# Attention ahead of the mixers instead of among them, with key chunks taken in twos

## The chip, the cores and the metric

The kernel runs on one core of a Trainium2 chip. The metric is the device time of one execution in microseconds. TensorE (PE) does matrix products into PSUM, VectorE (DVE), ScalarE (ACT) and GpSimd (POOL) work on elements, and SP's queue issues most DMAs.

## The reference

Four batches, eight heads, 768 queries and keys of 64 elements; then a mixer over tokens and channels.

```python
q_assign = np.argmax(np.einsum('bhsd,hcd->bhsc', q_n, c_n), axis=-1)
k_assign = np.argmax(np.einsum('bhsd,hcd->bhsc', k_n, c_n), axis=-1)
mask = q_assign[:, :, :, None] == k_assign[:, :, None, :]
scores = np.where(mask, scale * np.matmul(q, k.transpose(0, 1, 3, 2)), -1000000000.0)
attn = np.exp(scores - np.max(scores, axis=-1, keepdims=True))
attn = attn / (np.sum(attn, axis=-1, keepdims=True) + 1e-09)
x = np.matmul(attn, v)            # then (B,H,S,D) -> (B, S, H*D), D = 512
h = np.maximum(x.transpose(0, 2, 1) @ w_tok1, 0.0) @ w_tok2     # 768 -> 256 -> 768
u = x + h.transpose(0, 2, 1)
out = u + np.maximum(u @ w_ch1, 0.0) @ w_ch2                    # 512 -> 1536 -> 512
```

Here q_n, k_n and c_n are q, k and the 16 centroids of each head, each scaled to length one. The mixer's weights arrive as 64-bit floats, of which the kernel reads two 32-bit words.

## The kernel before

The work unit of attention is a pair `g`: one batch and two heads, 16 pairs in all. `load(g)` brings q and k of the pair in 32 DMAs of 24 KB and v in one, all on SP's queue and two pairs ahead. `turn` (L242) transposes q and k on VectorE into `qkT`, `route_products` (L251) multiplies them with the centroids, `route` (L264) finds each row's first greatest centroid as a one-hot row, and `route_turn` (L291) transposes these on TensorE into `ohT`.

A pair has 12 steps: two halves of the queries (384 columns) by six chunks of 128 keys. A step's `scores` (L312) adds two products into one PSUM tile `sc`: the one-hot rows of queries and keys in bf16, scaled so that a pair of different clusters gets -2**33, and the f32 scores. The two heads lie in two halves of the array's rows (64x128 tiles). ScalarE makes the exp `ex`. Two steps later `values` (L328) multiplies `ex` with v into `av`, the two heads in two halves of the array's columns (128x64 tiles), and VectorE adds `ex` to `sum`. There are two `sc` tiles of two banks each. At a half's end `normalise` (L354) sums over the partitions with a product by ones (`den`), takes the reciprocal of all 128x384 elements, multiplies the transposed output `xT` with it, and GpSimd gathers the largest sums and reciprocals in `worst`. `turn_x` (L374) transposes `xT` on TensorE into `x`.

The mixer of a batch is cut into items. When the four pairs of a batch are done, its items go into `fill`, and `gap()` issues some of them after each later attention step, so that mixer b runs among the steps of batch b+1; the last mixer runs alone. `tok1` (L409) and `tok2` (L423) are the token products, `ch1` (L438) and `ch2` (L452) the channel products; `ch2` adds u by products with an identity (L459).

The weights come in 31 pieces, 512 or 384 KB each, one or two per step from the start. `weight_round` (L162) makes f32 of the two words in five VectorE operations, one of ScalarE and two of GpSimd.

At the end a count of partitions in which sums and reciprocals stayed in range is loaded into the engines' registers; a branch goes to a general version of the kernel if any did not. On this data it isn't taken.

The order in which each engine gets its instructions is the order in which the code is written.

## Time and profile before

| | us |
|---|---|
| runs of the kernel before | median 1219.48 (1219.26 to 1219.65, 3 runs) |
| profiled execution | 1218.17 |
| its span, first to last instruction | 1216.4 |
| TensorE busy | 1046.0 |
| VectorE busy | 532.8 |
| ScalarE busy | 253.2 |
| GpSimd busy | 199.5 |

The profiled execution is one run; what lies outside the span (1.8 us) is launch and end. Busy times of engines overlap in time. TensorE's clock has two levels, 1.2 and 2.4 GHz; the granted clock of a stretch is its mean, 1.00 for the higher one throughout.

### The profile page before, as it was taken

The numbers are of one execution on the slowest core, as the hardware profiler recorded it, in microseconds if no ns is written. First come the engines' busy times: TensorE is split into PE (matmuls) and PEld (weight loads), VectorE is DVE, ScalarE is ACT, GpSimd is POOL, SyncE is SP. The second block draws the span as 40 slices with busy tenths as digits, with TensorE's granted clock in tenths as the row PEclk, the third lists the DMA queues.
The fourth block names the chain that finished last, engine by engine and source line by source line (L and its number), as shares of the span: only waits on it lengthen the run. The fifth ranks groups of instructions, "written<-read, shape, count | busy, mean of one in ns | idle before, by whom it ended". The sixth has DMA issues, their size and how long they took to land.

```text
span 1216.4 us, 10935 instructions
## 1 busy us (share of the span) xinstructions
PE 1046.0 (86%) x4227; PEld 461.8 (38%) x4227; DVE 532.8 (44%) x639; ACT 253.2 (21%) x374; POOL 199.5 (16%) x168
## 2 busy tenths in 40 slices
PE   0425344589999999999999999999999999999997
PEld 0102111133444444444444444444444444455553
DVE  3459989988443325333444334344433243120000
ACT  0212212144222122212222122222221221000000
POOL 0135646522011001011111111110110011000000
PEclk9767667699999999999999999999999999999999
DMA  2342332232020011021100020121000000000000
GB/s 48 109 117 86 80 115 87 61 62 47 11 39 1 26 28 26 1 57 35 30 10 22 9 48 1 24 51 19 14 1 16 11 1 1 26 1 9 18 1 29
DMA packets 118972, 41.74 MB, mean 34 GB/s; under 512 B 107776, under 2 KB 111872, under 8 KB 118912
## 3 DMA queue, kind: packets, MB, share of 16 engines
q1 hardware_dynamic: 118912, 40.96, 14.0%
q8 instruction: 35, 0.57, 0.2%
q14 instruction: 25, 0.20, 0.0%
HBM read 34.64 MB, written 6.29 MB: 34 GB/s over the span
## 4 chain that ended last, share of the span: by engine, by line
PE 73%; DVE 12%; SPq 10%; ACT 2%; DMA 1%; issue 1%; DVEq 0%; ACTq 0%
PE pc L438 21%; PE po L452 21%; PE sc L320 10%; SPq L132 9%; PE av L336 8%; PE pu L423 4%; PE ph L409 3%; DVE wh L175 2%; DVE wh L178 2%; PE po L459 2%; DVE sum L347 1%; DVE wT L188 1%; PE den L362 1%; DVE wh L183 1%; PE px L381 1%
## 5 line engine op out<-in xcount | busy, mean ns | idle before, releaser
L438 PE MATMUL pc<-xT,wc 128*128 128x384 f32 x768 | 265.0, 493 | 0.0
L452 PE MATMUL po<-wc,h 128*128 128x512 f32 x576 | 260.9, 600 | 0.0
L325 ACT ACTIVATE ex<-sc 128x768 f32<-128x768 f32 x192 | 155.4, 810 | 441.7 <-PE sc L320 439.9
L438 PEld LDWEIGHTS pc<-xT,wc 128*128 128x128 f32 x768 | 140.2, 190 | 114.4 <-issue 26.4
L336 PE MATMUL av<-ex,va 128*64 128x384 f32 x768 | 175.1, 536 | 0.0
L320 PE MATMUL sc<-qkT 64*128 64x384 f32 x768 | 168.2, 518 | 0.0
L452 PEld LDWEIGHTS po<-wc,h 128*128 128x128 f32 x576 | 104.9, 190 | 134.0 <-issue 133.5
L347 DVE TENSOR_TENSOR sum<-sum,ex 128x768 f32<-128x768 f32 x128 | 140.1, 1094 | 18.2 <-ACT ex L325 13.8
L371 POOL TENSOR_TENSOR worst<-worst,rcp 128x384 f32<-128x384 f32 x32 | 42.9, 1339 | 632.4 <-DVE rcp L366 632.4
L389 DVE TENSOR_SCALAR h<-pc 128x384 f32<-128x384 f32 x48 | 26.7, 557 | 236.6 <-PE pc L438 236.6
L366 DVE RECIPROCAL rcp<-den 128x384 f32<-128x384 f32 x32 | 81.8, 2556 | 97.9 <-PE den L362 97.9
L320 PE MATMUL sc<-ohT 64*128 64x384 bf16 x384 | 68.6, 353 | 23.2 <-ACT ex L325 22.6
L336 PEld LDWEIGHTS av<-ex,va 128*64 128x64 f32 x768 | 39.2, 139 | 112.9 <-issue 109.6
L370 POOL TENSOR_TENSOR worst<-worst,sum 128x384 f32<-128x384 f32 x64 | 67.2, 1050 | 88.0 <-DVE sum L347 85.5
L320 PEld LDWEIGHTS sc<-qkT 64*128 64x128 f32 x768 | 75.8, 206 | 0.9 <-issue 0.9
L320 PEld LDWEIGHTS <-ohT 64*128 64x128 bf16 x384 | 19.3, 94 | 136.0 <-issue 133.0
L197 POOL TENSOR_TENSOR wlow<-wlow,wpow 128x512 f32<-128x512 f32 (+1 forms) x31 | 47.0, 1516 | 134.5 <-DVE wpow L192 73.7
L257 PE MATMUL pr<-qkT,cnd 128*32 128x384 f32 x128 | 16.3, 584 | 49.5 <-DVE qkT L246 49.5
L391 ACT ACTIVATE h<-pc 128x384 f32<-128x384 f32 x48 | 23.6, 491 | 165.8 <-PE pc L438 165.8
L381 PE MATMUL px<-ident,xT 128*128 128x128 f32 x96 | 18.4, 304 | 39.1 <-DVE xT L368 26.6
L196 ACT ACTIVATE wlow<-raw 128x512 f32<-128x512 uint32 (+1 forms) x31 | 20.4, 658 | 138.3 <-POOL wc L201 77.2
L175 DVE TENSOR_SCALAR wh<-raw 128x512 uint32<-128x512 uint32 (+1 forms) x31 | 34.8, 1123 | 32.7 <-DMA raw<-in_moe_w_tok_dram 27.6
(68 smaller groups left out, 626.1 us busy)
## 6 DMA issues: line engine op xcount, KB each, us to landing
raw<-in_moe_w_ch_dram SPq DMA_DIRECT2D x24, 512.0 KB, 3.6
qk<-in_q_dram SPq DMA_DIRECT2D x256, 24.0 KB, 2.2
qk<-in_k_dram SPq DMA_DIRECT2D x256, 24.0 KB, 2.2
va<-in_v_dram SPq DMA_DIRECT2D x16, 384.0 KB, 3.3
out_dram<-o SPq DMA_DIRECT2D x24, 256.0 KB, 2.0
raw<-in_moe_w_tok_dram SPq DMA_DIRECT2D x3, 512.0 KB, 5.7
raw<-in_moe_w_tok_dram SPq DMA_DIRECT2D x4, 384.0 KB, 3.2
cen<-in_centroids_dram SPq DMA_DIRECT2D x1, 32.0 KB, 1.8
```

Of the source, the lines that this page charges most:

```text
L132: nc.sync.dma_start(d4[:, i], s4[:, i])
L175: nc.vector.tensor_scalar(out=h, in0=hi, scalar1=0x7FFFFFFF, scalar2=None, op0=ALU.bitwise_and)
L197: nc.gpsimd.tensor_tensor(out=low, in0=low, in1=power.bitcast(F32), op=ALU.mult)
L320: nc.tensor.matmul(sc[:, h, 0:HS], lhsT=src[rows, 1, j], rhs=src[rows, 0, js], start=start, stop=not start,)
L325: nc.scalar.activation(out=ex, in_=sc[:, :, 0:HS], func=ACT.Exp, scale=SM_SCALE)
L336: nc.tensor.matmul(st["av"][h * D : (h + 1) * D], lhsT=st["va"][:, h, j], rhs=ex[:, h], start=(j == 0), stop=(j == NJ - 1),)
L347: nc.vector.tensor_tensor(out=acc, in0=acc, in1=st.pop(("ex", qh, j)), op=ALU.add)
L366: nc.vector.reciprocal(out=rcp, in_=den)
L370: nc.gpsimd.tensor_tensor(out=worst[0], in0=worst[0], in1=acc[:, h], op=ALU.add)
L423: nc.tensor.matmul(pu, lhsT=st["h1"][:, t, f * P : (f + 1) * P], rhs=wt2[:, t, js], start=(t == 0), stop=(t == NT - 1),)
L438: nc.tensor.matmul(pc, lhsT=wc1[:, f, ct * P : (ct + 1) * P], rhs=uT[:, f, HJ * hf : HJ * hf + HJ], start=(f == 0), stop=(f == NF - 1),)
L452: nc.tensor.matmul(st["pf"], lhsT=st["h2"][:, ct, j * P : (j + 1) * P], rhs=wc2[:, ct], start=(ct == 0), stop=False,)
```

## The change

All 16 pairs of attention now come first, then the four mixers one after another. The parts:

- A step is a group `m` of two key chunks (96 groups, six per pair): both chunks' scores, which fill both `sc` tiles, then both chunks' values of two groups before. `work` has 7 `ex` buffers instead of 5.
- `av` is copied once (`avT`) and transposed by `half_turn`; `half_out` divides where `px` leaves PSUM, straight into `x`. Row sums come as 32-row tiles (`half_sums`), VectorE transposes them, and `half_reciprocals` takes 128x6 elements.
- `route` compares with the row's greatest value alone; that each row has one winner is counted in `cells`, from `route_turn`, whose copies both go to ScalarE. `worst` and its sums on GpSimd are gone; `fits` tests the reciprocals after the first batch's mixer and loads three counts there.
- q and k of a pair come in eight DMAs of 96 KB; for the first pair q's go on ScalarE's queue.
- Rounding a weight piece takes three VectorE operations, two of ScalarE and one of GpSimd. One piece is done every four groups; the 12 pieces of `w_ch2` come after attention, beside the first mixer's `ch1`, in memory that attention has left.
- All four batches' `x` are kept. The first batch's `tok1` and `tok2` stand at the end of attention (`ends`). `tok2` adds into `x`, `turn_u` transposes u for `ch1`, and `ch2` adds u on VectorE instead of by identity products. The next batch's token products stand inside the last channel products of the one before.

```diff
-STEPS = 2 * NJ
+GROUPS = NJ
+WEVERY = 4
...
-LAG_V, LAG_D = 2, 4
...
-    def pool(name, bufs, **kw):
-        return fast.enter_context(tc.tile_pool(name=name, bufs=bufs, **kw))
...
-    ps_sc = pool("ps_sc", 2, space=PSUM)
+    def pool(name, bufs, stack=None, **kw):
+        return (stack or fast).enter_context(
+            tc.tile_pool(name=name, bufs=bufs, reuse_waits="tile", **kw)
+        )
+    ps_w = pool("ps_w", 3, space=PSUM)
     ps_av = pool("ps_av", 1, space=PSUM)
-    ps_m = pool("ps_m", 2, space=PSUM)
...
+    ps_sc_stack = fast.enter_context(ExitStack())
+    ps_sc = pool("ps_sc", 2, ps_sc_stack, space=PSUM)
...
+    work = pool("work", 7, attention)
...
+    def load(g, queues=None):
...
-        for a, src in enumerate((q, k)):
+        for a, src in ((1, k), (0, q)):
+            queue = queues[a] if queues else nc.sync
...
-                d4 = st["qk"][c * QP : (c + 1) * QP, a].rearrange("r j i d -> r i j d")
-                for i in range(NQ):
-                    nc.sync.dma_start(d4[:, i], s4[:, i])
+                queue.dma_start(
+                    st["qk"][c * QP : (c + 1) * QP, a].rearrange("r j i d -> r (j i) d"),
+                    src[b, h, :, d0 : d0 + QP].rearrange("(i r j) d -> r j i d", i=NQ, j=NJ),
+                )
...
+        def scalar_part(p):
+            p["h"] = tmp("wh", U32, p["n"])
+            nc.scalar.activation(out=p["h"].bitcast(F32), in_=p["hi"].bitcast(F32), func=ACT.Abs)
+            p["up"] = tmp("wup", I32, p["n"])
+            nc.scalar.activation(out=p["up"], in_=p["lo"], func=ACT.Copy, scale=float(2.0**-29))
...
+            nc.vector.tensor_scalar(
+                out=h.bitcast(F32), in0=h.bitcast(F32), scalar1=TINY, scalar2=HUGE,
+                op0=ALU.max, op1=ALU.min,
+            )
+            nc.vector.tensor_scalar(
+                out=h, in0=h, scalar1=0x07FFFFFF, scalar2=3,
+                op0=ALU.bitwise_and, op1=ALU.logical_shift_left,
+            )
+            T = tmp("wT", U32, p["n"])
+            nc.vector.scalar_tensor_tensor(
+                out=T, in0=p["hi"], scalar=0xC0000000, in1=h,
+                op0=ALU.bitwise_and, op1=ALU.bitwise_or,
+            )
...
+            nc.gpsimd.tensor_tensor(out=dst.bitcast(I32), in0=T, in1=up, op=ALU.add)
...
+        for i in range(len(pieces) + 2):
+            def step(i=i):
+                if 2 <= i:
+                    rest(pieces[i - 2][0], parts[i - 2])
+                if 1 <= i <= len(pieces):
+                    scalar_part(parts[i - 1])
+                if i < len(pieces):
+                    load_bits(pieces[i][1], parts[i])
+            yield step
...
-        ge = small.tile([P, NR, C], F32, name="ge")
-        nc.vector.tensor_tensor(
-            out=ge, in0=sc, in1=mx.unsqueeze(2).to_broadcast([P, NR, C]), op=ALU.is_ge
-        )
-        nc.vector.tensor_tensor(
-            out=ge, in0=ge, in1=ramp.unsqueeze(1).to_broadcast([P, NR, C]), op=ALU.mult
-        )
-        first = small.tile([P, NR], F32, name="first")
-        nc.vector.reduce_max(out=first, in_=ge, axis=AX.X)
         oh = ohs[g % 2].rearrange("p a j (h x) -> p (a j) h x", h=2)[:, :, :, 0:C]
         nc.vector.tensor_tensor(
-            out=oh, in0=ge.rearrange("p (n h) c -> p n h c", h=2),
-            in1=first.rearrange("p (n h) -> p n h", h=2).unsqueeze(3).to_broadcast([P, 2 * NJ, 2, C]),
-            op=ALU.is_equal,
+            out=oh, in0=sc.rearrange("p (n h) c -> p n h c", h=2),
+            in1=mx.rearrange("p (n h) -> p n h", h=2).unsqueeze(3).to_broadcast([P, 2 * NJ, 2, C]),
+            op=ALU.is_ge,
         )
...
-        if a == 0:
+        if a == 1:
...
         if a == 0:
             nc.scalar.copy(out=st["ohT"][:, 0], in_=po)
         else:
-            nc.vector.tensor_scalar(
-                out=st["ohT"][:, 1], in0=po, scalar1=BIG, scalar2=-BIG, op0=ALU.mult, op1=ALU.add
-            )
-    def split(n):
-        g, s = divmod(n, STEPS)
-        return g, s // NJ, s % NJ
-    def scores(n):
-        g, qh, j = split(n)
+            nc.scalar.activation(
+                out=st["ohT"][:, 1], in_=po, func=ACT.Copy, scale=BIG, bias=-BIG,
+                accum_out=cells[:, g : g + 1],
+            )
...
-        sc = ps_sc.tile([P, 2, 512], F32, name="sc")
+        scs = [ps_sc.tile([P, 2, 512], F32, name="sc") for _ in range(2)]
         for src, start in ((st["ohT"], True), (st["T"], False)):
+            for i in range(2):
+                for h in range(2):
+                    rows = slice(h * D, (h + 1) * D)
+                    nc.tensor.matmul(
+                        scs[i][:, h, 0:HS], lhsT=src[rows, 1, j0 + i], rhs=src[rows, 0, js],
+                        start=start, stop=not start,
+                    )
+        for i in range(2):
+            ex = work.tile([P, 2, HS], F32, name="ex")
+            nc.scalar.activation(out=ex, in_=scs[i][:, :, 0:HS], func=ACT.Exp, scale=SM_SCALE)
+            st["ex", qh, j0 + i] = ex
+    def add_up(m):
+        g, qh, j0 = split(m)
+        st = state[g]
+        e = [st["ex", qh, j0 + i] for i in range(2)]
+        if j0 == 0:
+            acc = st["sum", qh] = sums.tile([P, 2, HS], F32, name="sum")
+            nc.vector.tensor_tensor(out=acc, in0=e[0], in1=e[1], op=ALU.add)
+        else:
+            acc = st["sum", qh]
+            for i in range(2):
+                nc.vector.tensor_tensor(out=acc, in0=acc, in1=e[i], op=ALU.add)
+    def values(m):
+        g, qh, j0 = split(m)
+        st = state[g]
+        if j0 == 0:
+            st["av"] = ps_av.tile([P, HS], F32, name="av")
+        for j in (j0, j0 + 1):
+            ex = st.pop(("ex", qh, j))
...
+                    st["av"][h * D : (h + 1) * D], lhsT=st["va"][:, h, j], rhs=ex[:, h],
+                    start=(j == 0), stop=(j == NJ - 1),
                 )
...
+        if j0 == NJ - 2:
+            st["avT", qh] = sums.tile([P, HJ, P], F32, name="avT")
+            nc.scalar.copy(out=st["avT", qh].rearrange("p j t -> p (j t)"), in_=st.pop("av"))
+    def half_sums(hi):
+        g, qh = divmod(hi, 2)
+        st = state[g]
+        acc = st.pop(("sum", qh)).rearrange("p h (j t) -> p (h j) t", j=HJ)
+        den = st["den"] = ps_w.tile([P, 2 * HJ, QP], F32, tag="w", name="den")
+        for i in range(NQ):
+            rows = slice(i * QP, (i + 1) * QP)
+            nc.tensor.matmul(den[rows], lhsT=ones, rhs=acc[:, :, rows], start=True, stop=True)
+    def half_reciprocals(hi):
+        g, qh = divmod(hi, 2)
+        dt = small.tile([P, 2 * HJ, QP], F32, name="dent")
+        nc.vector.transpose(
+            out=dt.rearrange("p n r -> p (n r)"),
+            in_=state[g].pop("den").rearrange("p n r -> p (n r)"),
+        )
+        nc.vector.reciprocal(
+            out=rcps[:, hi].rearrange("p h j -> p (h j)"), in_=dt[:, :, 0]
+        )
...
+    def half_turn(hi):
+        g, qh = divmod(hi, 2)
+        st = state[g]
+        avT = st.pop(("avT", qh))
+        px = st["px"] = ps_w.tile([P, HJ, P], F32, tag="w", name="px")
+        for i in range(HJ):
+            nc.tensor.transpose(out=px[:, i], in_=avT[:, i], identity=ident)
+    def half_out(hi):
...
         b, f = divmod(g, NF)
...
+        nc.vector.tensor_tensor(
+            out=xs[b][:, HJ * qh : HJ * qh + HJ, f * P : (f + 1) * P].rearrange(
+                "p j (h d) -> p j h d", h=2
+            ),
+            in0=state[g].pop("px").rearrange("p j (h d) -> p j h d", h=2),
+            in1=rcps[:, hi].rearrange("p h j -> p j h").unsqueeze(3).to_broadcast([P, HJ, 2, D]),
+            op=ALU.mult,
+        )
...
+    h1 = h1pool.tile([P, NT, DM], F32, name="h1")
+    def tok1(b, t):
+        pf = mtile([P, DM], "ph1")
+        for j in range(NJ):
+            nc.tensor.matmul(
+                pf, lhsT=wt1[:, j, t * P : (t + 1) * P], rhs=xs[b][:, j],
+                start=(j == 0), stop=(j == NJ - 1),
+            )
+        relu(h1[:, t], pf)
+    def tok2(b, j):
+        pu = mtile([P, DM], "pu")
+        for t in range(NT):
+            nc.tensor.matmul(
+                pu, lhsT=wt2[:, t, j], rhs=h1[:, t], start=(t == 0), stop=(t == NT - 1)
+            )
+        nc.vector.tensor_tensor(out=xs[b][:, j], in0=pu, in1=xs[b][:, j], op=ALU.add)
...
+    def turn_u(b, hf):
+        uT = uTs[b, hf] = pools["mlp"].tile([P, NF, HJ, P], F32, name="uT", bufs=2)
+        for f in range(NF):
+            pt = ps_w.tile([P, HJ, P], F32, tag="w", name="pt")
+            for i in range(HJ):
+                nc.tensor.transpose(
+                    out=pt[:, i], in_=xs[b][:, HJ * hf + i, f * P : (f + 1) * P], identity=ident
+                )
+            nc.scalar.copy(out=uT[:, f], in_=pt)
...
+    def ch2(b, hf, i):
+        po = mtile([P, DM], "po2")
+        for ct in range(NCT):
+            nc.tensor.matmul(
+                po, lhsT=pools["h2"][:, ct, i * P : (i + 1) * P], rhs=pools["wc2"][:, ct],
+                start=(ct == 0), stop=(ct == NCT - 1),
+            )
+        u = xs[b][:, HJ * hf + i]
+        nc.vector.tensor_tensor(out=u, in0=po, in1=u, op=ALU.add)
+        nc.sync.dma_start(out[b].rearrange("(p j) m -> p j m", p=P)[:, HJ * hf + i], u)
...
+    def fits():
...
+        for i, (limit, op) in enumerate(((LIMIT, ALU.is_le), (1.0 / LIMIT, ALU.is_ge))):
+            nc.vector.tensor_scalar(
+                out=inside[:, i], in0=flat, scalar1=limit, scalar2=None, op0=op
+            )
+            nc.vector.tensor_reduce(out=good[:, i : i + 1], in_=inside[:, i], axis=AX.X, op=ALU.min)
...
+        loaded = [
+            nc.values_load(count[0:1, i : i + 1], min_val=0, max_val=P) for i in range(3)
+        ]
+        return loaded[0] + loaded[1] + loaded[2]
...
+        load(0, (nc.scalar, nc.sync))
...
+    weights = list(weight_steps(stage, ("tok", "ch1")))
+    last = NPAIR * GROUPS
+    HALF = GROUPS // 2
+    ends = [lambda t=t: tok1(0, t) for t in range(NT)] + [lambda j=j: tok2(0, j) for j in range(NJ)]
...
+    for m in range(last + 5):
+        g, s = divmod(m, GROUPS)
+        if half_at(m - 4) is not None:
+            half_out(half_at(m - 4))
+        if 1 <= m <= last:
+            add_up(m - 1)
+        if m < last:
+            scores(m)
+        if m == last:
+            ps_sc_stack.close()
+        if 2 <= m < last + 2:
+            values(m - 2)
+        if g < NPAIR - 1:
+            if s == 0:
                 turn(g + 1)
+            elif s == 1:
+                route_products(g + 1)
+            elif s == 2:
+                route(g + 1)
             elif s == 3:
-                route_products(g + 1)
+                route_turn(g + 1, 1)
             elif s == 4:
-                route(g + 1)
-            elif s == 7:
                 route_turn(g + 1, 0)
-            elif s == 8:
...
+        if s == 1 and g + 2 < NPAIR:
             load(g + 2)
...
+        if m % WEVERY == 0 and weights:
+            weights.pop(0)()
+        if half_at(m - 2) is not None:
+            half_sums(half_at(m - 2))
+        if half_at(m - 3) is not None:
+            half_reciprocals(half_at(m - 3))
+            half_turn(half_at(m - 3))
+        if m >= last:
+            if m == last:
+                pools["ps_m"] = pool("ps_m", 4, space=PSUM)
+            for _ in range(2):
+                if ends:
+                    ends.pop(0)()
+    assert not weights and not state
+    for item in ends:
         item()
+    attention.close()
...
+    weights = list(weight_steps(mstage, ("ch2",)))
+    for _ in range(3):
+        weights.pop(0)()
+    turn_u(0, 0)
+    for b in range(B):
+        for hf in range(2):
+            for ct in range(NCT):
+                ch1(b, hf, ct)
+                if weights:
+                    weights.pop(0)()
+                if hf == 0 and ct == 2:
+                    turn_u(b, 1)
+            nxt = b + 1 < B and hf == 1
+            if nxt:
+                for t in range(NT):
+                    tok1(b + 1, t)
+            for i in range(HJ):
+                ch2(b, hf, i)
+                if nxt and i == 0:
+                    for j in range(NJ):
+                        tok2(b + 1, j)
+                if nxt and i == 1:
+                    turn_u(b + 1, 0)
+        if b == 0:
+            both = fits()
```

What moves on TensorE and VectorE, as each gets its instructions (the operand at the left of the arrow is written; numbers tell tiles apart). TensorE before, in the middle of the program, where ch1 of one batch (`pc`) stands among attention steps of the next, one chunk per step (the second head's mask row is left out):

```order
L336 MATMUL av<-ex,va 64x384 x2
L438 MATMUL pc_1943<-xT,wc_105 128x384 x4
L320 LDWEIGHTS ohT
L320 MATMUL sc<-ohT 128x384
...
L320 MATMUL sc<-qkT 128x384 x2
L336 MATMUL av<-ex,va 64x384 x2
L438 MATMUL pc_1969<-xT,wc_105 128x384 x4
```

TensorE now, in the middle of attention, one group from mask to x turn:

```order
L340 LDWEIGHTS ohT_300
L340 MATMUL sc_556<-ohT_300 128x384
...
L340 MATMUL sc_557<-ohT_300 128x384
L340 MATMUL sc_556<-qkT_217 128x384 x2
L340 MATMUL sc_557<-qkT_217 128x384 x2
L369 MATMUL av_570<-ex_502,va_132 64x384 x2
L369 MATMUL av_570<-ex_504,va_132 64x384 x2
L404 MATMUL px_578<-ident_93,avT_539 128x128 x3
```

The mixer's products are gone from between, and two chunks' scores, then two chunks' values, stand together.

VectorE before, at the end of a query half while weights are rounded (`wh`, `wT`, `wpow`):

```order
L178 TENSOR_SCALAR wh<-wh 128x512
L183 TENSOR_SCALAR wh<-wh 128x512
L188 SCALAR_TENSOR_TENSOR wT<-raw,wh 128x512
L192 TENSOR_SCALAR wpow<-wT 128x512
L366 RECIPROCAL rcp<-den 128x384
L368 TENSOR_TENSOR xT<-xT,rcp 128x384
L347 TENSOR_TENSOR sum<-sum,ex 128x768
```

VectorE now, at such a place:

```order
L191 TENSOR_SCALAR wh<-wh 128x512
L196 TENSOR_SCALAR wh<-wh 128x512
L201 SCALAR_TENSOR_TENSOR wT<-raw,wh 128x512
L390 STREAM_TRANSPOSE dent<-den 128x192
L394 RECIPROCAL rcps<-dent 128x6
L410 TENSOR_TENSOR x_105<-px,rcps 128x3x128
L359 TENSOR_TENSOR sum<-sum,ex 128x768 x2
```

The long reciprocal has become a transpose and a reciprocal of six columns, and the product reads PSUM (`px`) and writes `x`.

TensorE now, where attention ends; before, these token products stood among the steps of the next pairs, as in the first piece:

```order
L369 MATMUL av_3410<-ex_3379,va_2942 64x384 x2
L369 MATMUL av_3410<-ex_3381,va_2942 64x384 x2
L439 MATMUL ph1_3433<-x0_105,wt1_102 128x512 x6
L439 MATMUL ph1_3441<-x0_105,wt1_102 128x512 x6
L369 MATMUL av_3410<-ex_3406,va_2942 64x384 x2
L369 MATMUL av_3410<-ex_3408,va_2942 64x384 x2
L385 MATMUL den_3455<-sum_3367,ones_95 32x192 x4
L448 MATMUL pu_3460<-h1_109,wt2_103 128x512 x2
L448 MATMUL pu_3464<-h1_109,wt2_103 128x512 x2
L404 MATMUL px_3471<-ident_93,avT_3453 128x128 x3
```

The first batch's token products have moved into the last pair's end.

## Rows read from the trace of the kernel before

**Rows 1.** Page, parts 1 and 2: engines; granted clock in 40 slices.

```profile
PE 1046.0 (86%) x4227; PEld 461.8 (38%) x4227; DVE 532.8 (44%) x639; ACT 253.2 (21%) x374; POOL 199.5 (16%) x168
...
PEclk9767667699999999999999999999999999999999
```

**Rows 2.** Windows: stretch, length, busy us by engine, granted clock, DMA share, GB/s.

```profile
90.00:150.00 60.00, 30.64 (x131) 10.15 (x127) 57.76 (x70) 16.47 (x25) 34.22 (x24) 0.67 0.31 90
...
270.00:330.00 60.00, 56.29 (x284) 22.66 (x281) 40.05 (x41) 19.61 (x27) 11.46 (x10) 1.00 0.18 31
...
500.00:700.00 200.00, 197.33 (x801) 85.19 (x800) 76.70 (x89) 42.37 (x61) 20.20 (x18) 1.00 0.12 25
```

**Rows 3.** Timeline, an attention step without mixer: start, us, engine, line, operation.

```profile
278.00 0.34 PE L320 MATMUL sc<-ohT 64*128 64x384 bf16 x2
...
278.17 0.81 PE L320 MATMUL sc<-qkT 64*128 64x384 f32 x4
...
278.91 0.87 PE L336 MATMUL av<-ex,va 128*64 128x384 f32 x4
279.03 0.81 ACT L325 ACTIVATE ex<-sc 128x768 f32<-128x768 f32 x1 [0.90 <-PE sc L320]
...
279.71 0.34 PE L320 MATMUL sc<-ohT 64*128 64x384 bf16 x2
```

**Rows 4.** Timeline: TensorE's other attention work, same stretch.

```profile
275.85 0.51 PE L299 MATMUL po<-identb,oh 128*128 128x128 bf16 x6
...
281.32 0.81 PE L362 MATMUL den<-sum,ones 128*64 128x384 f32 x4
...
285.48 0.55 PE L381 MATMUL px<-ident,xT 128*128 128x128 f32 x3
...
285.96 0.34 PE L320 MATMUL sc<-ohT 64*128 64x384 bf16 x2
...
289.96 0.85 PE L257 MATMUL pr<-qkT,cnd 128*32 128x384 f32 x8 [0.52 <-DVE qkT L246]
```

**Rows 5.** Chain that ended last, in order of time: start, us, what.

```profile
300.94 5.15 PE ph L409 x12
...
559.31 5.15 PE ph L409 x12
...
1079.75 30.96 PE pc L438 x96
1110.71 10.30 PE po L452 x24
```

**Rows 6.** VectorE groups: count, busy us, mean ns, idle before.

```profile
L347 DVE TENSOR_TENSOR sum<-sum,ex 128x768 f32<-128x768 f32 x128 | 140.1, 1094 | 18.2 <-ACT ex L325 13.8
L366 DVE RECIPROCAL rcp<-den 128x384 f32<-128x384 f32 x32 | 81.8, 2556 | 97.9 <-PE den L362 97.9
...
L178 DVE TENSOR_SCALAR wh<-wh 128x512 f32<-128x512 f32 x27 | 28.7, 1062 | 0.9
...
L188 DVE SCALAR_TENSOR_TENSOR wT<-raw,wh 128x512 uint32<-128x512 uint32 x27 | 18.7, 693 | 2.7
...
L270 DVE STREAM_TRANSPOSE sim<-pr 128x384 f32<-128x384 f32 x16 | 9.3, 579 | 19.8 <-PE pr L257 19.7
```

**Rows 7.** Timeline of the start; last row: issue of a weight load.

```profile
1.20 10.40 SPq L132 DMA_DIRECT2D qk<-in_q_dram  x16
...
23.60 1.84 DVE L246 STREAM_TRANSPOSE qkT<-qk 128x768 f32<-128x768 f32 x2 [16.75 <-DMA qk<-in_k_dram]
...
33.89 0.50 PE L320 MATMUL sc<-ohT 64*128 64x384 bf16 x2 [0.65 <-DVE ohT L303]
...
35.46 0.53 PE L320 MATMUL sc<-ohT 64*128 64x384 bf16 x2
...
59.89 0.33 SPq L159 DMA_DIRECT2D raw<-in_moe_w_tok_dram  x1
```

**Rows 8.** Timeline of the end.

```profile
1208.91 0.59 ACT L467 COPY o<-po 128x512 f32<-128x512 f32 x1 [21.80 <-PE po L459]
```

370 lines of the change are left out of this document (100 added, 270 removed).

## The prediction

> **What bounds the kernel now.** I read the page's first two parts first: TensorE is busy for 1046 of 1216.4 us, no other engine for more than 533, and the granted clock is below full for the first eight of 40 slices [rows 1]. The windows then split the span in two regimes. From 90 to 150 us VectorE is busy for 57.8 of 60 us and TensorE for 30.6, at a mean clock of 0.67: here VectorE sets the pace (weight rounding, sums, reciprocals) and TensorE waits. From 270 us on TensorE is busy for 94 to 99% at full clock and VectorE for 38 to 67% [rows 2]. So there are two places to gain: the first 300 us, and what TensorE itself does after them.
>
> The timeline of one attention step without mixer work shows what TensorE pays for a key chunk [rows 3]: scores begin at 278.00, values at 278.91, the next scores at 279.71, a period of 1.71 us. How much of it is streaming? In the last mixer, 96 records of 128x384 take 30.96 us [rows 5], 0.3225 each; an f32 matmul of the program is two records, 0.645. The two heads of a chunk run side by side in halves of the array, so a chunk should stream 0.16 (bf16 scores, a quarter) + 0.645 (f32 scores) + 0.645 (values) = 1.45. The other 0.26 sits at the two changes of tiling in each step, 64x128 to 128x64 and back. The start of the program supports this: there scores follow scores without a change, 1.57 us apart at half clock [rows 7], which is 0.79 at full clock, no more than the 0.81 of streaming.
>
> The chain of waits gives the period of a batch in the busy regime: the first token product starts at 300.94 and again at 559.31, so 258.4 us for four pairs of heads and one mixer [rows 5].
>
> **The change, part by part.** The new order has no shared regime, so I build the sum anew, stage by stage.
>
> *Start.* Before, 16 issues take 10.40 us, 0.65 each; after 32 of them and a landing the first turn begins at 23.60, the first scores at 33.89 [rows 7]. Now there are four issues for k on SP's queue and, beside them, four for q on ScalarE's, each four times the size. No row shows such an issue. Bounds: 0.33 us, what a 384 KB weight load's issue takes [rows 7], if size doesn't matter; 2.6 (four times 0.65) if the price goes by runs of 128 B. The first turn thus starts between 4 and 13 us; ScalarE's four issues also stand ahead of the square root that the centroids need, which can add some us at the upper price. I take 12, nearer the upper end because the runs are as short as those of the 0.65 row. From turn to scores it was 10.3; two operations of about 0.58 [rows 6] go from routing. First scores at about 22, bounds 14 and 26. The start at half clock costs some 2 us more.
>
> By the Trainium skill, "DMA: Bandwidth & Descriptors", section "Issuing engines are not separate DMA queues", starting transfers from several engines saves only the sequencer's issue time, usually small beside the transfer. The rows differ: 32 issues at 0.65 are 20.8 of the 22.4 us before the first turn.
>
> *Attention.* A group of two chunks streams 2 x 1.45 and changes twice: 3.16 us instead of 3.42. Per pair TensorE also has one routing product (0.85), two routing turns (0.51), two x turns (0.55) and two row-sum products, which shrink from 384 columns (0.81) to 192 on four column tiles, about 0.41 [rows 4]. These busy times overlap what follows: the x turn at 285.48 holds the next scores up for 0.48, not 0.55, and I take 0.07 off each of the seven. That gives 3.3 and 6 x 3.16 + 3.3 = 22.3 us per pair; 16 pairs, the last without routing (1.7), 355 us. If grouping saves nothing because weight loads stay exposed, 25 us more (96 x 0.26).
>
> Does another engine hold it up? VectorE per pair, at the busy regime's prices [rows 6]: ten sums of 1.094, two turns 1.84 together [rows 7], three routing operations of at most 0.58, twice a small transpose, a reciprocal of six columns and a product (at most 0.58 each), and 19/16 of a weight piece at 1.06 + 1.06 + 0.69. Sum at most 21.3. The 2.556 us reciprocals, two rounding operations and GpSimd's sums are gone. ScalarE: 12 x 0.81, four copies and 2.4 rounding passes at no more than 0.81, 14.9. SP: eight issues of 0.33 to 2.6 plus v and weights, 4 to 22. So all of it lies beside TensorE's 22.3; the cover is thin for VectorE (1.0) and at SP's upper price (nothing). Queued behind VectorE's new transposes are the sums, for whom the next row-sum product waits, but a group later. I allow 3 us of stalls.
>
> *The seam.* After the last scores TensorE has the first batch's token products to do while the last pair ends, so nothing idles there by plan. The second channel weights are now loaded and rounded after attention, beside the first 12 channel products of 30.96/12 = 2.58 us each [rows 5]. Per piece VectorE needs at most 2.8 and half a clamp, ScalarE at most 1.6 and half a clamp: VectorE's cover is just short at these prices, which the crowded first regime set. If the cover fails, each of 12 pieces costs up to 1 us. I take 5 with the first turn of u, bounds 1 and 15.
>
> *Mixers.* Per batch 2 x 30.96 and 6 x 10.30 [rows 5]; the two token products are each 24 records of the latter's shape, 10.3; the 24 transposes of u at 0.16 (0.48/3) replace the additions by identity (L459): 148 us, 593 for four. The same arithmetic for before, 4 x (12 x 1.71 + 4.1) + 144, leaves 15 of the 258.4 for the identity matmuls and a third change per step; the size is right.
>
> *The branch's count* moves from the end to the end of the first batch: all engines stop for VectorE's short chain and the loads of three registers. Nearest row: from the last copy's start to the span's end, with the output's DMA, 7.5 us [rows 8]. I take 5, and 7.5 for the end as before, which keeps DMA and branch.
>
> *Sum:* 22 + 2 + 355 + 3 + 5 + 593 + 5 + 7.5 = 992.5 us of span. The profiled execution took 1218.17 beside a span of 1216.4; with the same 1.8 outside, 994.3, say 995. The median of the runs is 1219.48, 0.1% above the profiled one; less than 0.2% is about what a measurement here can tell from no change.
>
> **Rivals.** *Two score tiles are too few.* A group fills both, so the next can't begin on the second until its exp is over; before, one was always free. The exp starts 1.03 us after its chunk's scores [rows 3]; in a group the first at 1.20, the second ends near 2.9, and TensorE wants that tile at 3.33. Against it: 0.4 to spare. For it: that margin must hold handover and every copy that delays an exp. Half a us per group is 48 us: about 1043.
>
> *VectorE becomes the bound.* Should its operations wait on one another in their order, 25 us per pair would give 43 more: 1038. For it: 21.3 of 22.3 at worst prices. Against it: those prices are means over a regime in which VectorE had a far longer queue.
>
> *The start is not shortened.* If the transfers and not their issues set when q and k are there, the first turn stays near 23 us, 11 more: 1006. For it: no row shows these bytes in eight issues. Against it: the 20.8 us of issues. The skill's rule above would give this case.
>
> *Attention at half clock, the case on the other side.* With no mixer work to fill gaps, TensorE could stall often enough to be held at the lower level, as at 90 to 150 us (0.67 at 51% busy). Streaming doubles, 6 x 6.06 + 5.9 = 42 us per pair, 320 more: 1315. It is slower than before once more than 70% of attention runs so. Against it: 270 to 330 us begins with attention alone and has 1.00 at 94% busy [rows 2], and at half clock TensorE would be busy nearly all the time, unlike in the slow windows.
> Of this the Trainium skill, "TensorE: Matmul & The Clock Gate", section "What's actually happening", says that throttled is the default and activity releases it; by that rule, and the rows agree, attention returns to full clock.
>
> **How the numbers follow.** Forecast 0.58 (973 to 1020; the lower bounds of start, half clock, stalls, seam and count take 22 off); start not shortened 0.12; score tiles 0.13; VectorE 0.08; half clock 0.04; the rest, nearly all with a gain, 0.05. To hold 8 in 10 the range goes from 973 to 1048, which takes in the first three cases, most of them. Faster has all but the half clock: 0.95; slower 0.04; same 0.01.
>
> **What would show it.** First scores at 14 to 26 us. Scores start 3.16 us apart in groups without other work, routing products 22.3 apart; TensorE busy for over 95% and clock 1.00 from 40 to 375 us, with VectorE near 85%. First token product near 378, the first channel product near 400, no gap of over 5 us before the second channel product; one gap of about 5 us after the first batch. I am wrong if TensorE waits in every group for an exp (score tiles), for sums (VectorE), or if the clock sinks in attention.

## The result and the profile after

The changed kernel takes 980.71 us (median of 4 runs, 979.81 to 981.73) beside 1219.37 for the kernel before on the same chip: a ratio of 0.8045, 95% interval 0.8031 to 0.8059. The forecast was 995 us, with a range of 973 to 1048. The profiled execution took 979.91 us; its span is 978.1.

The page's first two parts, of the changed kernel, answer to [rows 1]:

```profile
PE 953.1 (97%) x4227; PEld 461.8 (47%) x4227; DVE 364.5 (37%) x554; ACT 263.2 (27%) x421; POOL 48.8 (5%) x40
...
PEclk9999999999999999999999999999999999999999
```

TensorE is busy for 93 us less and has 97% of the span. Its granted clock is 9 tenths or more in every slice, where [rows 1] has a 6 or a 7 in seven slices (the second to the eighth; the prediction reads the first eight). The experiments below price two kinds of work that left TensorE. VectorE lost 168 us and GpSimd 151; both were busy beside TensorE, so that alone says nothing of the time.

Windows of the changed kernel (stretch, length, busy us by engine, granted clock, DMA share, GB/s): attention as a whole and a part of it, the first mixer's channel products, and two stretches around the count before the branch.

```profile
40.00:375.00 335.00, 335.00 (x2409) 147.16 (x2406) 254.80 (x368) 191.17 (x287) 29.55 (x19) 1.00 0.33 74
200.00:300.00 100.00, 100.00 (x729) 44.03 (x725) 81.04 (x118) 58.24 (x89) 11.82 (x7) 1.00 0.41 92
402.00:440.00 38.00, 36.41 (x116) 20.58 (x115) 24.42 (x36) 15.46 (x28) 14.31 (x11) 1.00 0.37 111
540.00:551.00 11.00, 7.14 (x19) 3.06 (x18) 2.19 (x9) 0.00 (x0) 0.00 (x0) 1.00 0.06 24
552.00:555.00 3.00, 3.00 (x6) 1.46 (x6) 0.00 (x0) 0.00 (x0) 0.00 (x0) 0.50 0.00 0
```

In attention TensorE has no gap from 40 to 375 us, where [rows 2] had it half idle; VectorE is at 76% there and at 81% from 200 to 300. The two regimes are one. The 402 to 440 row holds the seam's gap, 38 less 36.41. The last two are the count: 3.86 us without TensorE, and soon after, from 552 to 555, 3 us in which it is busy throughout but granted 0.50, the lower of its two levels. From 557 to 600 it is granted 1.00 again.

The start, from the timeline, answers to [rows 7]:

```profile
0.74 2.87 ACTq L133 DMA_DIRECT2D qk<-in_q_dram  x4
...
4.94 0.20 ACT L234 ACTIVATE nrm<-lo 128x1 f32<-128x1 f32 x1
...
8.17 0.39 DVE L258 COPY cnd<-cnT 64x64 f32<-64x64 f32 x2
...
8.59 1.84 DVE L267 STREAM_TRANSPOSE qkT<-qk 128x768 f32<-128x768 f32 x2
...
16.45 0.82 PE L340 MATMUL sc<-ohT 64*128 64x384 bf16 x4 [1.04 <-ACT ohT L318]
```

One issue takes 0.72 us (2.87/4), hardly more than the 0.65 of an issue a quarter as large in [rows 7]. The first turn, at 8.59, comes right behind the centroids' last copy and waits for neither q nor k. The first scores come at 16.45 instead of 33.89.

One pair of heads, from the timeline: its routing products, SP's issues, a group without other work, and the next pair's routing products.

```profile
200.44 0.85 PE L278 MATMUL pr<-qkT,cnd 128*32 128x384 f32 x8
...
201.50 4.48 SPq L133 DMA_DIRECT2D qk<-in_k_dram  x4
...
206.01 2.77 SPq L133 DMA_DIRECT2D qk<-in_q_dram  x4
...
216.50 0.50 PE L340 MATMUL sc<-ohT 64*128 64x384 bf16 x4
...
217.69 1.51 ACT L346 ACTIVATE ex<-sc 128x768 f32<-128x768 f32 x2 [1.84 <-PE sc L340]
...
219.66 0.50 PE L340 MATMUL sc<-ohT 64*128 64x384 bf16 x4
...
222.82 0.85 PE L278 MATMUL pr<-qkT,cnd 128*32 128x384 f32 x8
```

The period of a pair is 22.38 us, that of a plain group 3.16. SP issues a pair's q and k in 7.3 us of it. The second exponential of the group ends at 219.20; the group that follows begins at 219.66 and its first two records, 0.17 in all, go to the other tile, so that the second tile is wanted near 219.83: 0.63 us of reserve.

The chain that ended last, in order of time (start, us, what):

```profile
373.14 10.50 PE ph L439 x24
...
536.40 10.32 PE po L479 x24
...
585.09 30.90 PE po L479 x72
...
689.59 10.30 PE po L479 x24
...
732.30 30.90 PE po L479 x72
```

From 536.40 to 585.09 it is 48.7 us; the same work a batch later, 689.59 to 732.30, takes 42.7. The count with all that follows from it thus costs 6.0 us: 3.9 of stop, and most of the rest the low clock: in the same chain the 24 records of channel products right behind the stop (from 550.75) take 9.67 us, and their like a batch later (from 699.89) 7.74.

What TensorE waited for, over the whole run (in total, times, longest):

```profile
PE pn L504 <- DVE good L502: 2.3, 1, 2.3
...
PE pc L470 <- issue: 1.6, 1, 1.6
PE pt L460 <- ACT uT L463: 1.6, 1, 1.6
```

After the start these three and one wait of 0.7 are all. The third is the seam; the timeline shows where it comes from:

```profile
406.49 0.67 ACT L184 ACTIVATE wh<-raw 128x512 f32<-128x512 f32 x1 [1.80 <-DMA raw<-in_moe_w_ch_dram]
...
407.61 1.60 ACT L463 COPY uT<-pt 128x384 f32<-128x384 f32 x4
```

The copies of u's second turn stand on ScalarE behind a rounding operation that waits 1.8 us for its weights, and TensorE's turns wait for their tiles. The mixers run at the prices of [rows 5], back to back.

**Where 238.3 us of span went.** First scores 17.4 us earlier (33.89 to 16.45). The first four pairs took 267.1 us before (33.89 to 300.94) and take 4 x 22.38 = 89.5 now: 177.5. The other 43.4 lie in twelve pairs, four mixers and the end; the experiments below price them.

### The profile page after: what moved, and what is told of

It is laid out like the page before. It is cut to its first block, busy times and chain, and to the rows that moved or that the text cites. A ratio compares the mean times of both kernels' runs of the same rounds, so it can differ in the third digit from the quotient of the medians.

```text
span 978.1 us, 10328 instructions
## 1 busy us (share of the span) xinstructions
PE 953.1 (97%) x4227; PEld 461.8 (47%) x4227; DVE 364.5 (37%) x554; ACT 263.2 (27%) x421; POOL 48.8 (5%) x40
## 4 chain that ended last, share of the span: by engine, by line
PE 97%; DVE 1%; ACT 1%; DMA 0%; issue 0%; ACTq 0%; DVEq 0%; SPq 0%
PE po L479 25%; PE pc L470 25%; PE sc L340 17%; PE av L369 14%; PE pu L448 4%; PE ph L439 4%; PE px L404 2%; PE po L316 1%; PE pr L278 1%; PE den L385 1%; PE pt L460 1%; DMA raw<-in_moe_w_ch_dram 0%; ACTq L133 0%; DVE qkT L267 0%; DVE x L484 0%
## 5 line engine op out<-in xcount | busy, mean ns | idle before, releaser
L470 PE MATMUL pc<-uT,wc 128*128 128x384 f32 x768 | 251.4, 489 | 1.6 <-issue 1.6
L470 PEld LDWEIGHTS pc<-uT,wc 128*128 128x128 f32 x768 | 146.3, 191 | 104.0 <-issue 6.1
L369 PE MATMUL av<-ex,va 128*64 128x384 f32 x768 | 145.1, 499 | 0.0
L340 PE MATMUL sc<-qkT 64*128 64x384 f32 x768 | 140.7, 486 | 0.0
L429 ACT ACTIVATE h<-pc 128x384 f32<-128x384 f32 x48 | 23.6, 492 | 359.2 <-PE pc L470 359.2
L340 PE MATMUL sc<-ohT 64*128 64x384 bf16 x384 | 48.5, 329 | 1.8 <-ACT ohT L318 1.0
L208 POOL TENSOR_TENSOR wc<-wT,wup 128x512 int32<-128x512 int32 x24 | 35.5, 1480 | 259.8 <-DVE wT L201 143.3
L448 PE MATMUL pu<-h,wt 128*128 128x512 f32 x96 | 42.1, 593 | 0.0
L439 PE MATMUL ph<-x,wt 128*128 128x512 f32 x96 | 42.0, 593 | 0.0
L355 DVE TENSOR_TENSOR sum<-ex 128x768 f32<-128x768 f32 x32 | 30.2, 944 | 6.3 <-ACT ex L346 5.7
L267 DVE STREAM_TRANSPOSE qkT<-qk 128x768 f32<-128x768 f32 x32 | 29.3, 953 | 0.0
L439 PEld LDWEIGHTS ph<-x,wt 128*128 128x128 f32 x96 | 18.2, 190 | 22.4 <-issue 21.6
```

Source lines behind the costliest of these rows:

```text
L208: nc.gpsimd.tensor_tensor(out=dst.bitcast(I32), in0=T, in1=up, op=ALU.add)
L267: nc.vector.transpose(out=st["T"][:, a].rearrange("p j t -> p (j t)"), in_=st["qk"][:, a].rearrange("p j i d -> p (j i d)"),)
L340: nc.tensor.matmul(scs[i][:, h, 0:HS], lhsT=src[rows, 1, j0 + i], rhs=src[rows, 0, js], start=start, stop=not start,)
L355: nc.vector.tensor_tensor(out=acc, in0=e[0], in1=e[1], op=ALU.add)
L369: nc.tensor.matmul(st["av"][h * D : (h + 1) * D], lhsT=st["va"][:, h, j], rhs=ex[:, h], start=(j == 0), stop=(j == NJ - 1),)
L439: nc.tensor.matmul(pf, lhsT=wt1[:, j, t * P : (t + 1) * P], rhs=xs[b][:, j], start=(j == 0), stop=(j == NJ - 1),)
```

## The experiments

All are timed against the kernel before on the same chip; its medians there were 1218.5 to 1219.2 us. Line numbers shift by a few where an edit adds lines.

**One chunk per change of tiling.** Scores and values of a chunk alternate again; all else as changed.

```diff
-        scs = [ps_sc.tile([P, 2, 512], F32, name="sc") for _ in range(2)]
-        for src, start in ((st["ohT"], True), (st["T"], False)):
-            for i in range(2):
+        for i in range(2):
+            sc = ps_sc.tile([P, 2, 512], F32, name="sc")
+            for src, start in ((st["ohT"], True), (st["T"], False)):
...
+            if 2 <= m:
+                values(m - 2, i)
```

> The changed kernel with one edit undone: one key chunk per change of tiling (scores of one chunk, values of one chunk, and again). Theory A, a change of tiling costs 0.13 us and each chunk's pair of changes 0.26: 96 more pairs of changes, 25 us more, about 1005.7 us, scores 1.71 us apart again. Rival B, the 0.26 was weight loads that stay exposed for each chunk however they are grouped: no change, about 981. Rival C, two score tiles filled at once cost the grouped order a wait: below 981.

Measured: 1004.32 us, ratio 0.8240 (0.8226 to 0.8254): 23.6 us over the changed kernel. The timeline shows the old step again, with no wait in it:

```profile
201.51 0.34 PE L340 MATMUL sc<-ohT 64*128 64x384 bf16 x2
...
203.22 0.34 PE L340 MATMUL sc<-ohT 64*128 64x384 bf16 x2
```

1.71 us, as in [rows 3]. So 23.6/96 = 0.25 us per pair of changes, where 0.26 was derived. The Trainium skill, "TensorEngine Tiling (Array Packing)", section "Key Properties", says that a change of tiling mode drains TensorE. The price here agrees with that, but the run doesn't tell a drain from weight loads that can't run ahead across a change.

**The first transfers on one queue.** q's four issues follow k's on SP's queue.

```diff
-        load(0, (nc.scalar, nc.sync))
+        load(0)
```

> The changed kernel with the first pair's q issued behind its k on SP's queue. In the trace after, an issue of 96 KB takes 0.72 to 0.75 us and the first turn starts at 8.59, right behind the centroids' last operation. Theory A, the issues set the start: q is there 2.9 us later, the first scores 1 to 3 us later (17.5 to 19.4 instead of 16.45), 982 to 984 us. Rival B, the transfers and not their issues set it: start and time as they are, 981.

Measured: 980.36 us, ratio 0.8046 (0.8033 to 0.8059): no difference. The timeline of this run:

```profile
3.29 0.20 ACT L234 ACTIVATE nrm<-lo 128x1 f32<-128x1 f32 x1 [1.27 <-DVE lo L232]
...
8.99 0.98 DVE L267 STREAM_TRANSPOSE qkT<-qk 128x768 f32<-128x768 f32 x1 [1.06 <-DMA qk<-in_q_dram]
...
15.99 0.82 PE L340 MATMUL sc<-ohT 64*128 64x384 bf16 x4 [1.04 <-ACT ohT L318]
```

q lands later, but ScalarE's square root no longer stands behind four issues (3.29 us, 4.94 with them), and the scores start 0.46 us earlier. The second queue bought nothing: it saved q's wait for four issues on SP, and held the square root, and all that follows from it, up by 1.65 us. The Trainium skill, "DMA: Bandwidth & Descriptors", section "Issuing engines are not separate DMA queues", says that starting transfers from several engines saves only the issue time. The prediction set the rows of before against that rule. The second queue agrees with it; the number of issues, which the next run changes, is another matter.

**32 small transfers.** Each of the eight is cut into four again (24 KB), on the two queues.

```diff
-                queue.dma_start(
-                    st["qk"][c * QP : (c + 1) * QP, a].rearrange("r j i d -> r (j i) d"),
-                    src[b, h, :, d0 : d0 + QP].rearrange("(i r j) d -> r j i d", i=NQ, j=NJ),
-                )
...
+                for i in range(NQ):
+                    queue.dma_start(d4[:, i], s4[:, i])
```

> The changed kernel with q and k of a pair in 32 DMAs of 24 KB again (first pair still on two queues). Theory A, price 0.65 us an issue, so only the start suffers: the first turn near 16 us instead of 8.6, and the second pair's turn waits for its load until about 35 us, in sum 12 to 17 us more, 993 to 998; later pairs keep 22.4 us, since 21.7 us of issues per pair still fit. Rival B, SP's queue becomes the bound of all of attention: pairs of 23 us or more, 1003 or more. Rival C, fewer DMAs bring nothing: 981.

Measured: 1009.09 us, ratio 0.8274 (0.8260 to 0.8288): 28.4 more. Its timeline:

```profile
16.32 1.84 DVE L267 STREAM_TRANSPOSE qkT<-qk 128x768 f32<-128x768 f32 x2
...
34.20 11.34 SPq L136 DMA_DIRECT2D qk<-in_k_dram  x16
...
35.69 1.51 PE L278 MATMUL pr<-qkT,cnd 128*32 128x384 f32 x8 [5.59 <-DVE qkT L267]
...
84.63 0.66 ACT L184 ACTIVATE wh<-raw 128x512 f32<-128x512 f32 x1 [6.04 <-DMA raw<-in_moe_w_tok_dram]
...
86.59 0.50 PE L340 MATMUL sc<-ohT 64*128 64x384 bf16 x2 [3.20 <-ACT ex L346]
```

The first turn comes 7.7 us later, and so does ScalarE's square root (at 12.67, 4.94 in the changed kernel): it now stands behind 16 issues that take 10.60 us. The rest is not in the start. SP issues for 11.34 us (k) and, from 45.59, 10.66 (q), with 1.1 for v and a weight; that is about 23 a pair beside TensorE's 22.38. Of TensorE's waits only the second pair's 5.59 us is for q and k. Eleven others, 10.6 us in all, are for exponentials, and the rows at 84.63 and 86.59 show the longest: the weights are issued behind q and k and land late, ScalarE's rounding waits for them, and an exponential stands behind the rounding. In two places the granted clock falls as well (0.82 from 24 to 40 us, 0.77 from 80 to 95). Fewer transfers were worth more than the start; the prediction had SP's cover at nothing only at the upper price of the large ones. With those SP needs 7.3 us for a pair's q and k.

**The kernel before, with the shorter rounding alone.** Three operations of VectorE for a weight piece, two of ScalarE and one of GpSimd.

```diff
-        nc.vector.tensor_scalar(
-            out=h, in0=hi, scalar1=0x7FFFFFFF, scalar2=None, op0=ALU.bitwise_and
-        )
+        nc.scalar.activation(out=h.bitcast(F32), in_=hi.bitcast(F32), func=ACT.Abs)
+        up = tmp("wup", I32)
+        nc.scalar.activation(out=up, in_=lo, func=ACT.Copy, scale=float(2.0**-29))
...
-        nc.vector.tensor_scalar(
-            out=power, in0=T, scalar1=0xFF800000, scalar2=None, op0=ALU.bitwise_and
-        )
```

> The kernel before, in which the rounding of one part takes three VectorE operations (and two of ScalarE, one of GpSimd) in place of four and a copy; nothing else is changed. Theory A: in the stretch without mixers (33.9 to 300.9 us of the kernel before) VectorE is what TensorE waits for, so VectorE's saved work comes off the time, about 27 x (1.21 + 0.43) + 4 x (0.55 + 0.36) = 48 us over the run of which most lies in the stretches where it is waited for: 30 to 48 us less, 1171 to 1190 us. Theory B: the mixers need their rounded weights, and the attention steps set no end beside them; TensorE's own total sets the time: 0 to 10 us less. Theory C: the new chain over ScalarE and GpSimd is longer than the old one and delays the weights: slower than 1219 us.

Measured: 1176.44 us, ratio 0.9647 (0.9631 to 0.9663): 42.7 less. In its chain the first token product stands at

```profile
260.12 5.15 PE ph L401 x12
```

against 300.94 in [rows 5]: 40.8 of the 42.7 us lie in the first 300. The rounding was what TensorE waited for there. The run also takes one of two operations off GpSimd; but in the kernel before it is VectorE that is busy for 57.8 of the 60 us from 90 to 150 [rows 2], and the page's chain that ended last holds no work of GpSimd, so the gain is put down to VectorE.

**The rounding packed.** A piece in every group of attention and not in every fourth.

```diff
-WEVERY = 4
+WEVERY = 1
```

> The changed kernel with a piece of the weights rounded in every group of attention, so that all of the first 19 pieces fall into the first 21 groups, and not into every fourth. Theory A: VectorE has 16.1 us per pair without rounding and 1.71 per piece, so 26.4 us in these pairs beside TensorE's 22.4; 4.0 us per pair for 3.5 pairs are lost: 14 us, 991 to 999 us. Theory B: the order of VectorE's queue has enough reserve: 980 to 984 us. Theory C: the dense stretch goes back to the first regime of the kernel before, with waits in chains and the clock down: 1010 us or more.

Measured: 996.28 us, ratio 0.8169 (0.8156 to 0.8181): 15.6 more, 14 expected. A window of this run in the dense stretch, and two rows of its timeline:

```profile
40.00:60.00 20.00, 17.66 (x131) 7.61 (x131) 18.84 (x32) 13.27 (x23) 5.20 (x4) 1.00 0.65 159
```

```profile
72.88 1.22 PE L278 MATMUL pr<-qkT,cnd 128*32 128x384 f32 x8 [2.26 <-DVE qkT L267]
...
101.85 0.85 PE L278 MATMUL pr<-qkT,cnd 128*32 128x384 f32 x8 [2.25 <-DVE qkT L267]
```

VectorE is at 94% and TensorE at 88%; a pair, by its routing products in the timeline above, takes 29.0 us there, the ones before and after it 27.5 and 25.2, and from 127 us on each takes 22.38 again. The total is as expected; the single pair isn't (26.4). When the weights are rounded over all of attention, VectorE never gets there. How much the order by itself would bring (mixers put back among the pairs in the changed kernel) was not tried: the mixers' PSUM and weights take the room that attention has left.

**A second long reciprocal.** A reciprocal of 128x384 is added on VectorE for each half; nothing reads it.

```diff
+        junk = small.tile([P, HS], F32, name="junk", bufs=1)
+        nc.vector.reciprocal(out=junk, in_=st_avT(hi).rearrange("p j t -> p (j t)"))
```

> The changed kernel with one more VectorE operation per query half, a reciprocal of 128x384 elements whose result is not used: the price of dividing before the transpose, 2.56 us each. In the trace after VectorE is busy for 18.1 of 22.4 us per pair. Theory A, with 5.1 us more VectorE would be the bound of attention (23.2 and waits in between): pairs of 23.3 to 24.5 us, 15 to 30 us more, 996 to 1011. Rival B, TensorE stays the bound because work can shift between groups: under 4 us more.

Measured: 987.53 us, ratio 0.8104 (0.8091 to 0.8118): 6.8 more, between the two theories. Routing products of this run in the timeline, and its waits:

```profile
227.28 0.85 PE L278 MATMUL pr<-qkT,cnd 128*32 128x384 f32 x8 [1.41 <-DVE qkT L267]
249.66 0.85 PE L278 MATMUL pr<-qkT,cnd 128*32 128x384 f32 x8
273.51 0.85 PE L278 MATMUL pr<-qkT,cnd 128*32 128x384 f32 x8 [1.41 <-DVE qkT L267]
```

```profile
PE pr L278 <- DVE qkT L267: 8.9, 7, 2.8
```

81.04 us of VectorE in 100 are 18.1 per pair in the changed kernel; two reciprocals of 2.515 make it 23.2, just past TensorE's 22.38. The period here is (273.51 - 227.28)/2 = 23.1, VectorE's own sum, with a wait in every second pair. There are six of these waits, growing from 0.25 us to 1.41, 6.1 us together (8.9 less the 2.8 of the start), and they are most of the 6.8. So 80 us of added work cost 6.8, and the cover of VectorE in the changed kernel is 4.3 us per pair in the mean, not the 1.0 of the prediction.

**Later exponentials.** Two idle copies on ScalarE between the two exponentials of each group; what they write is unused.

```diff
+            if i == 0:
+                idle = small.tile([P, 2 * HS], F32, name="idle", bufs=1)
+                flat = st["T"][:, 0].rearrange("p j t -> p (j t)")
+                nc.scalar.copy(out=idle, in_=flat)
+                nc.scalar.copy(out=idle[:, 0:HS], in_=flat[:, 0:HS])
```

> The changed kernel with two copies on ScalarE added between the two exponentials of each group (768 and 384 columns, about 0.75 + 0.48 = 1.23 us; what they write is unused). Theory A: two score tiles leave 0.63 us between the end of the second exponential and the matmul that needs it in the plain group (3.16 us), and up to 1.5 us in the groups with other work; so about 0.6 us is lost in a plain group, 0.2 us in each of three others, 1.2 us per pair, 19 us in all: 1000 us (996 to 1004). Theory B: the tiles have enough reserve, nothing is lost: 980 to 983 us. Theory C: the exponentials limit the group already, and all of it is lost, 96 x 1.23 = 118 us: about 1099 us.

Measured: 1010.66 us, ratio 0.8300 (0.8279 to 0.8321): 29.9 more where 19 (15 to 23) were expected, and far from all of the delay (118). Its timeline, a plain group and three routing products (in the order of time the latter come first):

```profile
48.55 0.85 PE L278 MATMUL pr<-qkT,cnd 128*32 128x384 f32 x8
72.34 0.85 PE L278 MATMUL pr<-qkT,cnd 128*32 128x384 f32 x8
96.67 0.85 PE L278 MATMUL pr<-qkT,cnd 128*32 128x384 f32 x8
...
213.10 0.34 PE L340 MATMUL sc<-ohT 64*128 64x384 bf16 x2
213.96 0.34 PE L340 MATMUL sc<-ohT 64*128 64x384 bf16 x2 [0.52 <-ACT ex L346]
```

TensorE now stops between the two score tiles, as the rival had it: the scores for the second wait 0.52 us for its exponential. Of the size, 1.2 us per pair was too little: an undisturbed pair (48.55 to 72.34) takes 23.8, 1.4 more, which makes 22.6 for 16. The next one takes 24.3. In it, and in every second pair while weights last, a rounding step of ScalarE falls into the group in which it also copies a routing turn, and an exponential comes later still; the expectation had not reckoned with that. Six such pairs (24.3 to 24.6) add 4.3 us, and the first whole pair, at 25.6, another 2.5. The reserve of two tiles is real and small.

**The identity additions put back.** u is added to po on TensorE, VectorE copies po. These are 96 matmuls, four for each of 24 output tiles (not three for 32, as the expectation counts them).

```diff
-                start=(ct == 0), stop=(ct == NCT - 1),
+                start=(ct == 0), stop=False,
+            )
+        for f in range(NF):
+            nc.tensor.matmul(
+                po[:, f * P : (f + 1) * P], lhsT=uTs[b, hf][:, f, i], rhs=ident,
+                start=False, stop=(f == NF - 1),
...
-        nc.vector.tensor_tensor(out=u, in0=po, in1=u, op=ALU.add)
+        nc.vector.tensor_copy(out=u, in_=po)
```

> The changed kernel with the identity matmuls of the second stage put back: u is added to po on TensorE, in three matmuls for each of 32 tiles, and VectorE copies po in place of adding. Theory A: TensorE sets the time of the mixers and has no gap there, so 96 matmuls of some 0.21 to 0.22 us are lost in full: 1001 to 1003 us. Theory B: they run where TensorE would wait: 980 to 985 us.

Measured: 1001.72 us, ratio 0.8218 (0.8204 to 0.8231): 21.0 more. From the timeline, one output tile's additions and the next tile's products:

```profile
442.43 1.05 PE L484 MATMUL po<-ident,uT 128*128 128x128 f32 x8
443.32 10.46 PE L479 MATMUL po<-wc,h 128*128 128x512 f32 x24
```

0.89 us each, 24 times: 21.4, in full on the path.

**Full-array work joined.** Both routing turns stand in one group, and each half's turn comes a group later, one of them right behind the routing turns. Four stretches of full-array work per pair become two, which is one pair of changes of tiling fewer.

```diff
-            elif s == 4:
                 route_turn(g + 1, 0)
...
-            half_turn(half_at(m - 3))
+        if half_at(m - 4) is not None:
+            half_turn(half_at(m - 4))
```

> The changed kernel with the full-array work of attention joined: the two transposes of the output of one pair and the transposes of x stand in one stretch, each half turned a group later, so that one pair of changes of tiling fewer is made for each pair of heads. Theory A: each pair of changes costs TensorE 0.26 us wherever it is: 16 x 0.26 = 4 us less, 976 to 977.5 us. Theory B: the changes hide behind waits for the exponentials in the groups with other work: 980 to 981 us. Theory C: the later turns come too late for the first mixer or hold a score tile: over 982 us.

Measured: 977.41 us, ratio 0.8019 (0.8005 to 0.8032): 3.3 less than the changed kernel, near the 4 of theory A. A pair, from routing products to routing products (199.35 and 221.48), takes 22.13 us instead of 22.38, so the pair of changes cost 0.25 here too. The timeline has the turns in one stretch:

```profile
206.78 0.84 PE L316 MATMUL po<-identb,oh 128*128 128x128 bf16 x12
207.46 0.50 PE L404 MATMUL px<-ident,avT 128*128 128x128 f32 x3
```

**And the count and the turn of u moved.** On top of it, VectorE's part of the count and its matmul go between channel products, and the second turn of u ahead of the rounding step.

```diff
+                if hf == 0 and ct == 2:
+                    turn_u(b, 1)
                 if weights:
                     weights.pop(0)()
-                if hf == 0 and ct == 2:
-                    turn_u(b, 1)
+                if b == 0 and hf == 1 and ct == 0:
+                    fits_inside()
+                if b == 0 and hf == 1 and ct == 6:
+                    fits_count()
...
-            both = fits()
+            both = fits_load()
```

> The kernel with the full-array work joined, and two more moves: the count before the branch is split (VectorE's part and the count's matmul go between channel products of the first batch's second half, only the register loads stay at the batch's end), and the second turn of u is issued ahead of the rounding step at the third channel product. Theory A: the two gaps of TensorE go, 1.59 us at the seam and 2.27 of the 3.9 us at the count (the loads of the registers still stop it, 1.6); joined took 3.3 off already: 972.5 to 974.5 us. Theory B: all of both gaps goes: 971 to 972.5 us. Theory C: the gaps move to the next wait: 977 to 978 us.

Measured: 969.26 us (5 runs, 968.88 to 969.72), ratio 0.7949 (0.7939 to 0.7960): the fastest version here, 11.5 us under the changed kernel, and more than theory B gave. Its rows at both places, the turn of u from the timeline and the stretch of the count from the windows:

```profile
393.53 0.93 PE L460 MATMUL pt<-ident,x 128*128 128x128 f32 x6 [0.24 <-ACT uT L463]
```

```profile
540.00:560.00 20.00, 20.00 (x69) 11.88 (x68) 2.36 (x4) 3.10 (x7) 0.00 (x0) 1.00 0.04 14
```

The seam's gap shrank from 1.59 to 0.24 us. At the count TensorE never stops, not for the register loads either, and the granted clock stays at 1.00: in the chain of this run the stretch that took 48.7 us in the changed kernel takes

```profile
531.69 10.30 PE po L479 x24
...
574.40 30.90 PE po L479 x72
```

42.7, the price of a batch without a count. So theory B's gaps went, and with them the clock's loss, which no theory had. The spans differ by 10.6 us: 2.9 with the work joined, 6.0 for the count, 1.35 at the seam, and 0.3 elsewhere.

## Why the prediction was right

The forecast case came, 14 us under its figure. All terms but the count's missed to the same side, so no two large misses hid each other. By its terms, in us of span:

| term | forecast | measured | from |
| --- | --- | --- | --- |
| start | 22 | 16.45 | first scores |
| attention, half clock, stalls | 360 | 356.7 | 16.45 to 373.14 |
| seam | 5 | 1.6 | wait for uT |
| mixers | 593 | 591.6 | the rest |
| count | 5 | 6.0 | the two batches' chains |
| end | 7.5 | 5.8 | last addition to span's end |
| sum | 992.5 | 978.1 | |

**Start: mis-sized by 5.5.** The step "I take 12, nearer the upper end because the runs are as short as those of the 0.65 row" failed: an issue of four times the bytes takes 0.72, not near 2.6. The first turn began at 8.59 and not at 12, right behind the centroids' last copy on VectorE. That is the wait the prediction named for the upper price (the square root behind ScalarE's issues). From the turn to the scores it was 7.9 us, not the 10 in the prediction's 22 (its own 10.3 less two operations of 0.58 gives 9.1). That four issues beside four are faster than eight in a row was wrong as a cause: the run on one queue is as fast. Fewer issues are what counted.

**Attention: right, by its mechanism.** 3.16 us for a plain group and 22.38 for a pair were derived as 3.16 and 22.3, and the run with one chunk per change gave back 23.6 of the 25 us. The 2 us for half clock at the start were not measured by themselves: the first four mask records take 0.82 us (16.45) and later ones 0.50 (216.50), though the granted clock of 15 to 20 us reads 1.00.

**Rivals.** Score tiles: a reserve of 0.63 us was enough, and TensorE waited 0.7 us once; the run with later exponentials shows that the mechanism exists and starts where that reserve ends. VectorE as bound: 18.1 us per pair, not 21.3. Some prices from the crowded regime were too high (the clamp, L191, takes 0.47 us where [rows 6] had 1.06), and the small transpose and reciprocal, put at 0.58 each, take 0.38 and 0.19. The prediction's 19/16 of a piece per pair is a mean over all 16 pairs; one piece in four groups is 1.5 per pair until they run out. The long reciprocal shows that VectorE does set the period once its sum is above 22.4. Start not shortened: refuted by 16.45. Half clock: the granted clock was 1.00 from 40 to 375 us.

**Seam and end, mis-sized by 3.4 and 1.7.** The step "VectorE's cover is just short at these prices" sized the seam: VectorE had 24.4 of 38 us there, and its cover held. What TensorE did wait for was ScalarE's copy, 1.6 us, and moving the turn of u took nearly all of that away. The end was taken from [rows 8] unchanged, although the count's register loads left it; 1.7 is about what those cost at the count (1.59), which was not tested by itself.

**The count: right in size.** It cost 6.0 where 5 stood, but in two parts, a stop of 3.9 us and 1.9 for the low clock after it; the prediction had only the stop.

**What was not forecast: where the 238 us come from.** The sum was made anew and gave none. By the runs: of the 177.5 us of the first four pairs, 40.8 are the shorter rounding alone; packing the short rounding costs 15.6 back. The rest, the long reciprocals, the clock below full and the mixer's weights all due before the first mixer, was not taken apart by a run. Of the other 43.4, the grouping in twelve pairs is 12/16 x 23.6 = 17.7 and the identity additions 21.0; 4.7 are left for the third change per step and the smaller row-sum products, less what is new: the two gaps and the turns of u, eight of 1.45 us in the chain. No run takes these apart. The prediction's check on the kernel before left 15.9 us a batch by its own figures (258.4 less 242.5), of which the identity matmuls are 5.3 by the run that puts them back; that the size is right is thus not shown.

## What to carry to other kernels

Build the sum from the engine that will be the only one without gaps, and price the others per period of it: 18.1 of 22.4 us was safe, 23.2 was not. Work that must precede a stage (here the weights' rounding) costs most when it is packed ahead of that stage's first use; spread over a stage with another bound it cost TensorE no gap. Where one engine is 97% busy, look for the small stops that are left, a branch's count or a copy queued behind others: their price can include the clock that follows, as at the count, and moving the producers earlier took 11.5 us here (with one change of tiling) and no other work removed.
